# First batch of an attention + MLP kernel: LN1's scale spread over the partitions in f32 instead of as split bf16, with the start-up work around it reordered

## The chip, the cores and the metric

The kernel runs on one core of one Trainium2 chip. The metric is the device time of one execution, in microseconds. The core has five engines that work through queues of their own and wait for each other by semaphores: TensorE (PE, matmuls; PEld is its weight load), VectorE (DVE), ScalarE (ACT), GpSimd (POOL) and SyncE (SP). [...] POOL's queue also issues most of the DMAs.

## The reference

Grouped-query attention (8 batches, 16 query heads, 4 key heads, 384 rows, 64 columns a head) is followed by an affine residual MLP over 1024 columns:

```python
attn = softmax(q @ k.T / sqrt(64)); x = (attn @ v) with heads side by side   # [8, 384, 1024]
a1 = alpha1 * x + beta1
tok = einsum('ts,bsd->btd', w_tok, a1)
u = x + lam * tok
a2 = alpha2 * u + beta2
ch = relu(a2 @ w_ch1) @ w_ch2          # 1024 -> 4096 -> 1024
out = u + lam * ch
```

## The kernel before, in words

**Stages.** Each batch has a *side* (attention, the token product `tok`, and the transpose of the result, `ut`) and a *main* part (the channel MLP: 32 column blocks `nt` of the first product `h`, line 399, then the second product `ch`, line 426). Batch 0's side runs alone at the start, up to 42 us. From then on the side of batch b + 1 is woven into the main part of batch b.

**Batch 0's side.** It is a list of small steps, built at lines 359 to 382: `scores(i)` for i = 0 to 17, and after each of them what the table `at` names for that i. The order written there is the order of the instructions on every engine's queue. `scores(i)` puts one 128 x 1024 block of q times k into a PSUM tile (tag "sc", two of them) and ACT takes its exponential (line 211). `av(p)` multiplies with v for a pair of heads p, and DVE normalises (`rinv`, `x`) and scales with `g1` (line 246), which gives `a1`. `tok(p)` multiplies `a1` with the transposed `w_tok`, adds a product `R` x `H` that carries beta, and DVE adds x (line 265). `ut(p)` transposes to `a2T`, and ACT empties that. PSUM tags "tp" and "av" have one buffer each and serve all the transposes, spreads and `rows_r`; "mm" has two.

**The vectors.** alpha1, beta1, alpha2 and lam come as rows of 128 columns on eight partitions, four copies of them (`rows_f`, 32 partitions, lines 471 to 473). alpha1 and beta1 are multiplied with lam (line 509). To copy a row to all 128 partitions, a matmul with a selector is used. For bf16 matmuls without loss, `split` (lines 505 to 517) takes each f32 row apart into three bf16 parts, one in each group of eight partitions, in five DVE operations (cast, subtract, cast, subtract, cast) that wait for one another. `spread` (line 313) is then four bf16 matmuls and one copy to `vecs`. `g1` is lam * alpha1, spread in two halves: `lower` for the first four column blocks, `upper` for the others. `fill_h` (line 520) lays lam * beta1's parts out as `H`, and `rows_r` (line 303) makes the row sums of `w_tok` as `R`.

**Loads.** `loads` (line 543) names the step of batch 0's side after which POOL's queue issues a load: after step 9 the fifth tile of W1 and the first half of W2's first 512 columns (2 MB of bf16), after step 20 the next k (on SP), after step 30 the next q, after step 37 the next v. A W1 tile is loaded again five tiles ahead (`RING`), when PE is done with the one whose place it takes; W2 otherwise comes in pieces during batch 0's main part (lines 413 to 417) and stays.

**The first product's evacuation in batch 0.** The product carries one more column, from which DVE takes the bias (line 405) of every block; then ACT (even blocks) or DVE (odd blocks) writes relu(h + bias) to `hT`. The first four blocks are begun inside batch 0's side (`h_part`), two to a PSUM tile.

The table of the order, as it was:

```python
at = {1: [(warmup, 3), (split, 0, 2, 0)], 2: [(q_transpose, 2, 2, "DVE", "av"), (split, 0, 2, 1)],
      3: [(spread, lower, (0, 1), "tp"), (wtok_transpose, 0, "av")],
      4: [(av, 0), (wtok_transpose, 1, "tp"), (wtok_transpose, 2, "av")], 5: [(fill_h,), (rows_r, "tp")],
      6: [(av, 1), (q_transpose, 4, 2)], 7: [(tok, 0), (k_transpose, 2)],
      8: [(av, 2), (spread, upper, (0, 1), "av")], 9: [(tok, 1), (ut, 0)], 10: [(av, 3), (ut, 1)],
```

The functions that the change touches:

Of the kernel before, what the change touches and what calls it, by code (L numbers as in the profile page):

```python
# [12 lines left out]
def kernel(  # L13
# [21 lines left out]
    nc = tc.nc  # L35
    f32 = mybir.dt.float32
# [3 lines left out]
    MUL = mybir.AluOpType.mult  # L40
    ADD = mybir.AluOpType.add

    B, Hq, S, D = q.shape
# [4 lines left out]
    P = 128  # L48
# [4 lines left out]
    NP = Hq // 2  # L53
# [3 lines left out]
    RING = 5  # L57
# [6 lines left out]
    psum = ST(tc.psum_pool(name="psum", bufs=2))  # L64
# [6 lines left out]
    g1, h1, al2, lam_t = (vecs[:, i] for i in range(4))  # L71
# [50 lines left out]
    def load_w1(n):  # L122
        if n < B * NCH:
            t = sb.tile([P, NDT, CW * P], bf, tag="w1", name="w1", bufs=RING)
            c = n % NCH
            nc.gpsimd.dma_start(out=t, in_=w1src[:, :, c * CW * P:(c + 1) * CW * P])  # L126
            w1_tiles[n] = t

    def load_w2(dw, i, n):
        r, cs = slice(i * NNT // n, (i + 1) * NNT // n), slice(dw * 512, (dw + 1) * 512)  # L130
        nc.gpsimd.dma_start(out=w2[:, r, cs], in_=w2src[:, r, cs])
# [6 lines left out]
    def evac(eng):  # L138
        return nc.scalar.copy if eng == "ACT" else nc.vector.tensor_copy
# [16 lines left out]
    def side(b):  # L156
# [156 lines left out]
        def spread(ps_, vs, tag, eng="DVE"):  # L313
# [3 lines left out]
            for i, p in enumerate(ps_):  # L317
# [2 lines left out]
            evac(eng)(out=vecs[:, vs[0]:vs[1], ps_[0] * P:(ps_[-1] + 1) * P].rearrange("p v (n d) -> p n v d", n=n),  # L320
                      in_=ps[:, :n * w].rearrange("p (n v) d -> p n v d", n=n))

        us = []

        def add(f, *a):
# [36 lines left out]
        lower, upper = range(NP // 2), range(NP // 2, NP)  # L362
        def av(p):
            av_piece(p, 0)
            av_piece(p, 1)

        ut = a2_transpose
        at = {1: [(warmup, 3), (split, 0, 2, 0)], 2: [(q_transpose, 2, 2, "DVE", "av"), (split, 0, 2, 1)],
              3: [(spread, lower, (0, 1), "tp"), (wtok_transpose, 0, "av")],
              4: [(av, 0), (wtok_transpose, 1, "tp"), (wtok_transpose, 2, "av")], 5: [(fill_h,), (rows_r, "tp")],  # L370
              6: [(av, 1), (q_transpose, 4, 2)], 7: [(tok, 0), (k_transpose, 2)],
              8: [(av, 2), (spread, upper, (0, 1), "av")], 9: [(tok, 1), (ut, 0)], 10: [(av, 3), (ut, 1)],
              11: [(q_transpose, 6, 2), (tok, 2)], 12: [(tok, 3)], 13: [(av, 4), (ut, 2)], 14: [(ut, 3)],
              15: [(tok, 4), (av, 5)], 16: [(ut, 4)], 17: [(av, 6), (tok, 5)]}
        for i in range(18):
            add(scores, i)
# [11 lines left out]
    def main(b):  # L388
        a2T = a2Ts[b % 2]
        x = xs.pop(b)  # L390
        n = S + 1 if b == 0 else S
        for c in range(NCH):
            w1 = w1_tiles.pop(b * NCH + c)
            for j in range(CW):
                nt = c * CW + j
                begun = b == 0 and nt in early
                ps = early[nt] if begun else psum.tile([P, 512], f32, tag="mm", name="h", bufs=2)
                for dt in range(0 if begun else NDT):
                    nc.tensor.matmul(out=ps[:, :n], lhsT=w1[:, dt, j * P:(j + 1) * P],  # L399
                                     rhs=a2T[:, dt, :n], start=(dt == 0), stop=(dt == NDT - 1))  # L400
                    if dt == 3:
                        yield T_H
                c1 = bias1[:, nt:nt + 1]
                if b == 0:
                    nc.vector.tensor_copy(out=c1, in_=ps[:, S:n])
                if nt % 2 == 0:
                    nc.scalar.activation(out=hT[:, nt, :], in_=ps[:, :S], func=RELU, bias=c1)  # L407
                else:
                    nc.vector.tensor_scalar(out=hT[:, nt, :], in0=ps[:, :S], scalar1=c1,  # L409
                                            scalar2=0.0, op0=ADD, op1=mybir.AluOpType.max)  # L410
                yield T_H
            load_w1(b * NCH + c + RING)
            if b == 0 and 2 <= c < 12:
                load_w2(*((0, 6 + c, 16) if c < 10 else (1, c - 10, 16)))
            if b == 0 and c == 12:
                for i in range(1, 8):
                    load_w2(1, i, 8)
        for dw in range(NDW):
            cs = slice(dw * 512, (dw + 1) * 512)
            for ms in range(NST):  # L420
                ps = psum.tile([P, 512], f32, tag="mm", name="ch", bufs=2)
                o = sb.tile([P, 512], f32, tag="tmp", name="o", bufs=4)
                last = (b, dw, ms) == (B - 1, NDW - 1, NST - 1)
                for lo, hi in ((0, 256), (256, 384), (384, 512)) if last else ((0, 512),):
                    for nt in range(NNT):
                        nc.tensor.matmul(out=ps[:, lo:hi], lhsT=hT[:, nt, ms * P:(ms + 1) * P],  # L426
                                         rhs=w2[:, nt, dw * 512 + lo:dw * 512 + hi], start=(nt == 0), stop=(nt == NNT - 1))
                        if nt % 4 == 3 and nt < NNT - 1:
                            yield T_C
                    c = slice(dw * 512 + lo, dw * 512 + hi)  # L430
                    nc.vector.tensor_tensor(out=o[:, lo:hi], in0=ps[:, lo:hi], in1=lam_t[:, c], op=MUL)  # L431
                    nc.vector.tensor_tensor(out=o[:, lo:hi], in0=o[:, lo:hi], in1=x[:, ms, c], op=ADD)  # L432
                    nc.sync.dma_start(out=out[b].rearrange("(p st) d -> p st d", st=NST)[:, ms, c], in_=o[:, lo:hi])
                yield T_C
# [4 lines left out]
    with tc.manual_schedule(engines=order):  # L439
# [12 lines left out]
        rows_f = hTf[:32, 9216:10240].bitcast(f32)  # L452
        rows_t = hTf[:32, 10240:11264].bitcast(f32)
        rows_b = hTf[:, 11264:11776]
# [5 lines left out]
        ident_f = hTf[:, 11776:12032].bitcast(f32)  # L460
        R = stage[:, 2120:2312].bitcast(bf)
        H = stage[:, 2312:2824].bitcast(bf)
        ones = stage[:, 2824:2840].bitcast(bf)
        masks = [stage[:32, 2840 + i:2841 + i] for i in range(3)]
        sel4 = stage[:32, 2844:2848].bitcast(bf)
# [5 lines left out]
        for i, ap in enumerate((moe_alpha1, moe_beta1, moe_alpha2, moe_lam)):  # L471
            nc.sync.dma_start(out=rows_f[:, i * P:(i + 1) * P],  # L472
                              in_=bass.AP(tensor=ap.tensor, offset=ap.offset, ap=[[0, 4], [P, NP], [1, P]]))
# [28 lines left out]
                nc.vector.tensor_reduce(out=t[:n], in_=ident[:n, :n].rearrange("p (k c) -> p c k", c=NP), op=ADD, axis=AX)  # L502


        def split(lo, hi, step=None):
            c = slice(lo * P, hi * P)
            if lo == 0 and step != 1:
                r = rows_f[:, c].rearrange("p (v d) -> p v d", v=2)
                nc.vector.tensor_tensor(out=r, in0=r, in1=rows_f[:, None, 3 * P:].to_broadcast([32, 2, P]), op=MUL)
            for i, m in enumerate(masks[:2]):  # L510
                if step in (None, i):
                    src, dst = (rows_t, rows_f) if i else (rows_f, rows_t)
                    nc.vector.tensor_copy(out=rows_b[:32, c], in_=src[:, c])
                    nc.vector.scalar_tensor_tensor(out=dst[:, c], in0=rows_b[:32, c], scalar=m, in1=src[:, c],
                                                   op0=MUL, op1=mybir.AluOpType.subtract)
            if step != 0:
                nc.vector.tensor_copy(out=rows_b[:32, c], in_=rows_f[:, c])


        def fill_h():  # L520
            nc.vector.tensor_tensor(out=H[:32].rearrange("p (n d) -> p n d", n=NP),
                                    in0=rows_b[:32, None, P:2 * P].to_broadcast([32, NP, P]),
                                    in1=sel4[:, :, None].to_broadcast([32, NP, P]), op=MUL)

        place_k(0, 0)
        for h, cp in ((0, nc.vector.tensor_copy), (2, nc.scalar.copy)):
# [13 lines left out]
        def late_loads():  # L540
            load_k(1)

        loads = {9: [(load_w1, RING - 1), (load_w2, 0, 0, 2)], 20: [(late_loads,)], 30: [(load_q, 1)], 37: [(load_v, 1)]}
        for i, f in enumerate(side(0)):
            f()
            for g, *a in loads.get(i, []):
                g(*a)
# [60 lines left out]
```

The softmax here doesn't subtract the row's maximum and nothing guards it: scores larger than these inputs give would overflow.

## Time and profile before

| What | us |
|---|---|
| Median of 8 runs (814.94 to 817.23) | 815.49 |
| The profiled execution | 815.17 |
| Its span, first to last instruction | 813.3 |
| PE busy in the span | 798.5 |
| DVE / ACT / POOL busy | 348.5 / 225.2 / 186.1 |
| Last matmul of `h_part`, end of batch 0's side | 42.0 |
| First matmul of `ch`, line 426 | 90.5 |

The profile is of one execution. Its span leaves out what lies before the first and after the last instruction, here 1.87 us. Busy times of engines overlap and don't add up. A line of the timeline gives start, length, engine, source line, operation, what is written and read, shapes, a count where neighbours are merged, and in brackets how long the engine had stood before and who released it. "Granted clock" is the share of TensorE's full clock that was given to it; 1.00 is full, 0.50 half.

### The profile page before, as it was taken

The numbers are of one execution on the slowest core, as the hardware profiler recorded it, in microseconds if no ns is written. First come the engines' busy times: TensorE is split into PE (matmuls) and PEld (weight loads), VectorE is DVE, ScalarE is ACT, GpSimd is POOL, SyncE is SP. The second block draws the span as 40 slices with busy tenths as digits, with TensorE's granted clock in tenths as the row PEclk, the third lists the DMA queues.
The fourth block names the chain that finished last, engine by engine and source line by source line (L and its number), as shares of the span: only waits on it lengthen the run. The fifth ranks groups of instructions, "written<-read, shape, count | busy, mean of one in ns | idle before, by whom it ended". The sixth has DMA issues, their size and how long they took to land.

```text
span 813.3 us, 14117 instructions
## 1 busy us (share of the span) xinstructions
PE 798.5 (98%) x6090; PEld 451.8 (56%) x6144; DVE 348.5 (43%) x678; ACT 225.2 (28%) x298; POOL 186.1 (23%) x230
## 2 busy tenths in 40 slices
PE   7999999999999999999999999999999999999997
PEld 4756555565556655566455654556555565456545
DVE  7655553344443444334452444424444244442122
ACT  4654330432113321233103331034211432102100
POOL 7244430224003240123301341022500321003000
PEclk8999999999999999999999999999999999999999
DMA  9999999999259992799947999489994998129611
GB/s 176 200 197 201 202 211 139 162 176 168 54 133 176 171 148 61 138 181 173 120 93 129 179 172 91 112 131 171 178 80 100 165 172 120 36 65 194 80 39 39
DMA packets 260670, 112.57 MB, mean 138 GB/s; under 512 B 109568, under 2 KB 254464, under 8 KB 260608
## 3 DMA queue, kind: packets, MB, share of 16 engines
q0 software_dynamic: 197760, 83.28, 90.7%
q1 hardware_dynamic: 62304, 28.00, 14.4%
q8 instruction: 48, 0.79, 0.4%
q10 hardware_dynamic: 544, 0.39, 0.2%
q14 instruction: 14, 0.11, 0.0%
HBM read 170.53 MB, written 12.58 MB: 225 GB/s over the span
## 4 chain that ended last, share of the span: by engine, by line
PE 94%; DVE 4%; issue 1%; DMA 0%; SPq 0%; ACT 0%; DVEq 0%; ACTq 0%
PE ch L426 41%; PE h L399 39%; PE av L236 5%; PE sc L202 4%; PE tok L258 4%; DVE hT L409 1%; DVE x L242 1%; PE h L150 1%; DVE a1f L249 0%; DVE a L251 0%; DMA hT<-in_moe_lam_dram 0%; PE ut L275 0%; ACT hT L407 0%; SPq L472 0%; PE vec L318 0%
## 5 line engine op out<-in xcount | busy, mean ns | idle before, releaser
L399 PE MATMUL h<-a2T,w 128*128 128x384 bf16 (+1 forms) x2016 | 349.8, 326 | 1.5 <-ACT hT L407 0.5
L426 PE MATMUL ch<-w,hT 128*128 128x512 bf16 (+2 forms) x1546 | 346.1, 370 | 4.4 <-issue 1.0
L399 PEld LDWEIGHTS <-w 128*128 128x128 bf16 x2016 | 189.4, 98 | 126.1 <-issue 9.6
L126 POOL DMA_DIRECT2D w<-in_moe_w_ch_dram x128 | 112.6, 880 | 542.7 <-PE h L399 500.0
L426 PEld LDWEIGHTS <-hT 128*128 128x128 bf16 x1600 | 146.1, 98 | 153.0 <-issue 5.8
L211 ACT ACTIVATE es<-sc 128x1024 bf16<-128x1024 f32 x126 | 123.4, 1021 | 283.2 <-PE sc L202 283.2
L409 DVE TENSOR_SCALAR hT<-h,bias 128x384 bf16<-128x384 f32 x128 | 79.0, 617 | 187.1 <-PE h L399 186.5
L407 ACT ACTIVATE hT<-h,bias 128x384 bf16<-128x384 f32 x128 | 74.4, 581 | 221.4 <-PE h L399 202.4
L431 DVE TENSOR_TENSOR o<-ch,vecs 128x512 f32<-128x512 f32 (+2 forms) x50 | 33.3, 667 | 91.1 <-PE ch L426 91.1
L265 DVE TENSOR_TENSOR x<-tok,x 128x384 f32<-128x384 f32 x64 | 35.5, 555 | 80.5 <-PE tok L258 76.9
L236 PEld LDWEIGHTS <-es 128*128 128x128 bf16 x1008 | 45.8, 97 | 20.5
L236 PE MATMUL av<-v,es 128*128 128x65 bf16 x1008 | 49.0, 193 | 0.0
L202 PE MATMUL sc<-qT,kT 64*128 64x384 bf16 (+2 forms) x576 | 45.9, 274 | 0.4 <-ACT hT L211 0.3
L258 PEld LDWEIGHTS <-wtokT 128*128 128x128 bf16 x576 | 37.8, 98 | 12.6 <-issue 0.6
L241 DVE RECIPROCAL rinv<-av 128x6 f32<-128x6 f32 x64 | 12.4, 193 | 69.0 <-PE av L236 68.6
L258 PE MATMUL tok<-a,wtokT 128*128 128x128 bf16 x504 | 37.3, 219 | 0.0
L242 DVE TENSOR_TENSOR x<-av,rinv 128x384 f32<-128x384 f32 x64 | 35.7, 557 | 2.3
L202 PEld LDWEIGHTS <-kT 64*128 64x128 bf16 x576 | 20.0, 94 | 28.9 <-issue 24.8
L432 DVE TENSOR_TENSOR o<-o,x 128x512 f32<-128x512 f32 (+2 forms) x50 | 35.0, 700 | 1.7
L269 DVE TENSOR_TENSOR a<-x,vecs 128x384 bf16<-128x384 f32 x56 | 31.4, 561 | 1.9
L251 DVE TENSOR_TENSOR a<-a1f,vecs 128x384 bf16<-128x384 f32 x56 | 31.2, 558 | 2.2
L249 DVE TENSOR_TENSOR a1f<-x,vecs 128x384 f32<-128x384 f32 x56 | 31.2, 558 | 1.9
(69 smaller groups left out, 211.5 us busy)
## 6 DMA issues: line engine op xcount, KB each, us to landing
w<-in_moe_w_ch_dram POOLq DMA_DIRECT2D x135, 512.0 KB, 7.4
out_dram<-o SPq DMA_DIRECT2D x47, 256.0 KB, 2.1
q_raw<-in_q_dram POOLq DMA_DIRECT2D x21, 256.0 KB, 8.5
kst<-in_k_dram SPq DMA_DIRECT2D x16, 192.0 KB, 2.7
w<-in_moe_w_ch_dram POOLq DMA_DIRECT2D x10, 256.0 KB, 11.8
w<-in_moe_w_ch_dram POOLq DMA_DIRECT2D x1, 2048.0 KB, 21.0
v<-in_v_dram POOLq DMA_DIRECT2D x21, 64.0 KB, 8.1
a2T<-a SPq DMA_TRANSPOSE x48, 4.1
```

The lines of the kernel that those rows point to most:

```text
L126: nc.gpsimd.dma_start(out=t, in_=w1src[:, :, c * CW * P:(c + 1) * CW * P])
L202: nc.tensor.matmul(out=sc[:, hh, k % 4:k % 4 + n], lhsT=kT[r, sk, 2 * p // G, :], rhs=qT[r, st:st + n, p, :], start=True, stop=True)
L211: nc.scalar.activation(out=e, in_=sc, func=EXP, scale=scale_qk)
L236: nc.tensor.matmul(out=av[:, hh, sq, :], lhsT=ess[k // 4][:, hh, k % 4, :], rhs=vb[:, sk, hk, :], start=(sk == 0), stop=(sk == NST - 1))
L242: nc.vector.tensor_tensor(out=x[:, :, cols(p)].rearrange("p st (h d) -> p h st d", h=2), in0=av[:, :, :, :D], in1=rinv.to_broadcast([P, 2, ...
L258: nc.tensor.matmul(out=ps[:, tt, :], lhsT=wtokT[:, st, tt * P:(tt + 1) * P], rhs=a1s[p][:, st, :], start=(st == 0), stop=(st == NST - 1 an ...
L265: nc.vector.tensor_tensor(out=u, in0=ps, in1=u, op=ADD)
L399: nc.tensor.matmul(out=ps[:, :n], lhsT=w1[:, dt, j * P:(j + 1) * P], rhs=a2T[:, dt, :n], start=(dt == 0), stop=(dt == NDT - 1))
L407: nc.scalar.activation(out=hT[:, nt, :], in_=ps[:, :S], func=RELU, bias=c1)
L409: nc.vector.tensor_scalar(out=hT[:, nt, :], in0=ps[:, :S], scalar1=c1, scalar2=0.0, op0=ADD, op1=mybir.AluOpType.max)
L426: nc.tensor.matmul(out=ps[:, lo:hi], lhsT=hT[:, nt, ms * P:(ms + 1) * P], rhs=w2[:, nt, dw * 512 + lo:dw * 512 + hi], start=(nt == 0), sto ...
L432: nc.vector.tensor_tensor(out=o[:, lo:hi], in0=o[:, lo:hi], in1=x[:, ms, c], op=ADD)
```

## The change

Five things are changed, all in batch 0:

1. `g1` is spread by a new function, `spread_g1`: four f32 matmuls with an f32 selector (a column of the identity) on the product rows themselves, with no split before it. `scale_rows` is the multiplication by lam alone.
2. `split` in batch 0 takes only lam * beta1 (128 columns instead of 256), in one go, after `av(0)` instead of before the first spread. The second batch still calls it for alpha2 and lam.
3. `fill_h` is made in two halves, after scores(5) and scores(8). `rows_r` and `k_transpose(2)` come after scores(7), before `tok(0)`; `tok(0)` after scores(8); other steps of the table shift by one place; the warm-up matmuls come after scores(0) instead of scores(1).
4. The bias copy of the first product alternates between ACT (even blocks) and DVE (odd blocks).
5. W2's first load is a quarter of the rows of its first 512 columns (1 MB) instead of half of them; the second quarter is issued after step 34, behind the next q and v, which were issued after steps 30 and 37.

```diff
+        def spread_g1(ps_, tag):
+            ps = psum.tile([P, 4, P], f32, tag=tag, name="vec", bufs=1)
+            for i, p in enumerate(ps_):
+                nc.tensor.matmul(out=ps[:, i], lhsT=ident_f[:NP, p:p + 1].to_broadcast([NP, P]),
+                                 rhs=rows_f[:NP, :P], start=True, stop=True)
+            nc.vector.tensor_copy(out=g1[:, ps_[0] * P:(ps_[-1] + 1) * P], in_=ps.rearrange("p n d -> p (n d)"))
...
-        at = {1: [(warmup, 3), (split, 0, 2, 0)], 2: [(q_transpose, 2, 2, "DVE", "av"), (split, 0, 2, 1)],
-              3: [(spread, lower, (0, 1), "tp"), (wtok_transpose, 0, "av")],
-              4: [(av, 0), (wtok_transpose, 1, "tp"), (wtok_transpose, 2, "av")], 5: [(fill_h,), (rows_r, "tp")],
-              6: [(av, 1), (q_transpose, 4, 2)], 7: [(tok, 0), (k_transpose, 2)],
-              8: [(av, 2), (spread, upper, (0, 1), "av")], 9: [(tok, 1), (ut, 0)], 10: [(av, 3), (ut, 1)],
-              11: [(q_transpose, 6, 2), (tok, 2)], 12: [(tok, 3)], 13: [(av, 4), (ut, 2)], 14: [(ut, 3)],
+        at = {0: [(warmup, 3)], 1: [(scale_rows,)], 2: [(q_transpose, 2, 2, "DVE", "av")],
+              3: [(spread_g1, lower, "tp"), (wtok_transpose, 0, "av")], 4: [(av, 0), (split, 1, 2), (wtok_transpose, 1, "tp")],
+              5: [(wtok_transpose, 2, "av"), (fill_h, 0)], 6: [(av, 1), (q_transpose, 4, 2)],
+              7: [(k_transpose, 2), (rows_r, "av")], 8: [(tok, 0), (av, 2), (fill_h, 4)],
+              9: [(spread_g1, upper, "av"), (tok, 1)], 10: [(ut, 0), (av, 3)],
+              11: [(q_transpose, 6, 2), (tok, 2), (ut, 1)], 12: [(tok, 3)], 13: [(av, 4), (ut, 2)], 14: [(ut, 3)],
...
-                    nc.vector.tensor_copy(out=c1, in_=ps[:, S:n])
+                    evac("DVE" if nt % 2 else "ACT")(out=c1, in_=ps[:, S:n])
...
+        def scale_rows():
+            r = rows_f[:, :2 * P].rearrange("p (v d) -> p v d", v=2)
+            nc.vector.tensor_tensor(out=r, in0=r, in1=rows_f[:, None, 3 * P:].to_broadcast([32, 2, P]), op=MUL)
...
+        def split(lo, hi):
             c = slice(lo * P, hi * P)
+            src, dst = rows_f, rows_t
+            for m in masks[:2]:
+                nc.vector.tensor_copy(out=rows_b[:32, c], in_=src[:, c])
+                nc.vector.scalar_tensor_tensor(out=dst[:, c], in0=rows_b[:32, c], scalar=m, in1=src[:, c],
+                                               op0=MUL, op1=mybir.AluOpType.subtract)
+                src, dst = dst, src
+            nc.vector.tensor_copy(out=rows_b[:32, c], in_=src[:, c])
...
+        def fill_h(p):
+            nc.vector.tensor_tensor(out=H[:32, p * P:(p + 4) * P].rearrange("p (n d) -> p n d", n=4),
+                                    in0=rows_b[:32, None, P:2 * P].to_broadcast([32, 4, P]),
+                                    in1=sel4[:, p:p + 4, None].to_broadcast([32, 4, P]), op=MUL)
...
-        loads = {9: [(load_w1, RING - 1), (load_w2, 0, 0, 2)], 20: [(late_loads,)], 30: [(load_q, 1)], 37: [(load_v, 1)]}
+        loads = {9: [(load_w1, RING - 1), (load_w2, 0, 0, 4)], 20: [(late_loads,)], 34: [(load_q, 1), (load_v, 1), (load_w2, 0, 1, 4)]}
```

The prediction's steps use these lines of the kernel before: 509 to 517 (`split`), 318 (`spread`), 488 and 98 (POOL's copies of q and k into place), 521 (`fill_h`), 309 and 310 (`rows_r`), 177 (`k_transpose`), 275 (`ut`), 405 to 410 (bias and `hT`).

More of the change, by code (lines that the diff above doesn't have):

```diff
@@ L502 @@
                 nc.vector.tensor_reduce(out=t[:n], in_=ident[:n, :n].rearrange("p (k c) -> p c k", c=NP), op=ADD, axis=AX)
-        def split(lo, hi, step=None):
+        def scale_rows():
+            r = rows_f[:, :2 * P].rearrange("p (v d) -> p v d", v=2)
+            nc.vector.tensor_tensor(out=r, in0=r, in1=rows_f[:, None, 3 * P:].to_broadcast([32, 2, P]), op=MUL)
+        def split(lo, hi):
             c = slice(lo * P, hi * P)
[L507 to L523, printed above, removed]
+            src, dst = rows_f, rows_t
[9 more added lines that the diff above has]
+                                    in1=sel4[:, p:p + 4, None].to_broadcast([32, 4, P]), op=MUL)
         place_k(0, 0)
```

## The prediction

> **What bounds the kernel now.** I read the page's busy table first, then its chain of waits.
>
> ```profile
> PE 798.5 (98%) x6090; PEld 451.8 (56%) x6144; DVE 348.5 (43%) x678; ACT 225.2 (28%) x298; POOL 186.1 (23%) x230
> ...
> PE 94%; DVE 4%; issue 1%; DMA 0%; SPq 0%; ACT 0%; DVEq 0%; ACTq 0%
> ```
>
> PE is busy 98% of 813.3 us. The edit touches only work before 92 us (the first batch's attention, up to 42.0 us, and its channel MLP's first product, 42.0 to 90.5 us), so it can win only PE's idle time there and can lose only there. The view by stages shows how much there is. Its columns are the stage and its length, the busy time (and instructions) of PE, PE weight loads, DVE, ACT and POOL, the granted TensorE clock, and the DMA share and rate.
>
> ```profile
> 8.97:12.38 3.41, 1.28 (x20) 0.89 (x17) 2.83 (x7) 2.13 (x3) 3.41 (x5) 1.00 1.07 179
> 12.38:15.79 3.41, 2.76 (x33) 1.85 (x30) 2.56 (x7) 1.71 (x2) 2.61 (x5) 0.50 1.41 169
> 15.79:19.21 3.42, 3.42 (x33) 1.94 (x34) 3.23 (x6) 1.37 (x2) 3.42 (x5) 0.50 1.45 197
> 22.62:42.00 19.38, 19.36 (x267) 14.12 (x265) 12.89 (x29) 13.27 (x18) 5.67 (x6) 1.00 1.52 195
> 42.00:54.00 12.00, 11.29 (x88) 6.88 (x87) 8.28 (x24) 3.77 (x7) 5.64 (x7) 1.00 1.64 199
> ```
>
> PE idles 2.1 us of 8.97 to 12.38. The clock then stands at 0.50 until 19.21, two stretches of 3.41 us. From 22.6 to 42 PE has no gap. From 42 to 54 it idles 0.7 us. Note DVE: from 15.79 to 19.21 it is busy 3.23 of 3.42.
>
> The timeline names the early wait and its neighbours (start, length, engine, line, operation).
>
> ```profile
> 7.02 0.56 POOL L529 DMA_DIRECT2D stage<-in_moe_w_tok_dram  x1
> 7.58 0.84 POOL L488 COPY q_raw<-qh 128x768 bf16<-128x768 bf16 x1
> 7.79 0.91 DVE L509 TENSOR_TENSOR hT<-hT 32x256 f32<-32x256 f32 x1 [0.43 <-DMA hT<-in_moe_lam_dram]
> 10.87 0.47 DVE L514 SCALAR_TENSOR_TENSOR hT<-hT,stage 32x256 f32<-32x256 bf16 x1
> 11.38 0.34 DVE L517 CAST hT<-hT 32x256 bf16<-32x256 f32 x1
> 11.77 0.38 PE L318 MATMUL vec<-hT,stage 128*128 128x128 bf16 x4 [2.05 <-DVE hT L517]
> 13.92 0.20 DVE L241 RECIPROCAL rinv<-av 128x6 f32<-128x6 f32 x1 [0.78 <-PE av L236]
> 14.15 0.83 POOL L488 COPY q_raw<-qh 128x768 bf16<-128x768 bf16 x1 [0.80 <-DMA qh<-in_q_dram]
> 14.92 1.29 POOL L98 CAST k<-kst 128x384 bf16<-128x384 f32 x2
> 15.85 1.44 DVE L521 TENSOR_TENSOR stage<-hT,stage 32x1024 bf16<-32x1024 bf16 x1
> 16.16 1.81 POOL L488 COPY q_raw<-qh 128x768 bf16<-128x768 bf16 x1
> 17.79 0.60 DVE L310 SCALAR_TENSOR_TENSOR stage<-hT,stage,r 32x384 bf16<-32x384 bf16 x1
> 20.41 0.50 PE L177 MATMUL tp<-ident,k 128*128 128x128 bf16 x6
> ```
>
> The split of alpha and beta (L509 to L517) ends at 11.72, and PE stands 2.05 us for it. But afterwards DVE runs almost without a gap to 20.4, and PE waits for what DVE empties (k_transpose(2) at 20.41 for the copy of qT that ends at 20.36).
>
> **The change, part by part.**
>
> *1. Spread without split.* L509's product stays (it ends at 8.70); the five split operations leave the path. The f32 spread can start behind scores(3), at 9.72. No f32 product is in the trace. Lower bound: the four bf16 products, 0.22 us in the chain. Nearest row: f32 transposes (L275), three in about 0.45, so 0.15 each and 0.6 for four. Upper bound: their weight load (141 ns) and matmul (273 ns) end to end, 1.65 for four. I take 0.6, so PE is free at 10.3. Next on PE is wtok_transpose(0). Its weight is issued at 7.02 and lands 4.2 us later, at 11.22; before, that was hidden. So it starts at 11.25, not at about 12.15, and the gain is 0.9 us of the 2.05. Scores(4) at 11.42 and av(0) at 11.75 to 12.4 run at full clock (PE is busy about 2.5 of 8.97 to 12.38). DVE's first reciprocal comes at 12.55 (before 13.92), and with 0.23 + 0.59 + 0.58 the scaled av(0) is ready at 13.95 (before 15.40). DVE is 1.45 us ahead here.
>
> [...]
>
> *2. DVE's queue behind it.* The split of beta now stands between av(0) and the copies of wtokT 1 and 2. Behind it wait q_transpose(4) (its PSUM buffer "tp" is wtokT 1's), then scores(7) behind that on PE, and so ACT. Five operations 128 wide: at 256 wide and undisturbed (50 to 52 us) the cast takes 0.28 and the subtraction 0.47, so 1.9 us with gaps at most and 0.9 at half; I take 1.4. They fall on POOL's copies from 14.15 to 17.97. L509 shows the price of that: 0.91 where the same width takes 0.47 in L514, because POOL's copy ran until 8.42; +0.44. Bounds: 0 if none collides, and 2.7 if four operations each wait for a copy (0.83, 0.65, 0.65, 0.83, less a start). I take three collisions, 1.3. The split ends at 13.95 + 1.4 + 1.3 = 16.65.
>
> [...]
>
> Then two wtokT copies 0.65 (17.3), half of fill_h, 1.44/2 (18.05), av(1)'s three 1.40 (19.45), the copy of qT 0.57 (20.0). k_transpose(2) on PE 0.33 and 0.2 to be seen (20.6), its copy 0.58 (21.2), rows_r's two 0.54 + 0.60 and gaps (22.4). So tok(0), moved behind k_transpose(2), rows_r and scores(8), starts at 22.45, not 19.50. Then PE still has tok(0) 0.64, av(2) 0.66 and the upper spread 0.6: 24.35. Before, the same list was done at 22.11 (the chain's scores after the spread). That is **+2.25**; with no collision +0.95, with all +3.65. PE was gapless from there on, so nothing wins it back.
>
> *3. The clock.* After a stretch with PE busy 1.28 of 3.41 the clock was 0.50; it stayed so through a stretch with 2.76 and rose after a full one. Now PE has only q_transpose(4) and scores(7), 0.66 us, between 15.79 and 19.21, so I expect 0.50 from 19.21, and, PE idling again until 22.45, to 26.04 if the stretches lie as before. At half clock av takes 1.12 for 0.66 and scores 0.54 for 0.33 (about 1.65 times): of 3.6 us 1.4 are lost. Bounds 0 and 1.4, I take half, **+0.7**.
>
> *4. First product of the MLP.* Even bias copies go to ACT, one DVE wait less in front of each ACT evacuation. The chain 42.03 to 46.02 (bias, hT, bias, hT and so on) holds PE 0.36 us at the end, q's late DMA (its half of W2's 2 MB is now behind it) 0.28, and the wait at 53.19 for an ACT evacuation behind the second split 0.46. All go: **-1.1**; bounds -0.3 (only q) and -1.4 (with the 0.3 at 71.65, which stays behind DVE's own queue). An ACT copy of one column is not in the trace: 0.58 for 384 and 1.02 for 1024 columns give a floor near 0.32, 16 times, hidden because PE needs the buffer two products (2.6 us) later. If that cover were gone, up to 16 x 0.15 = 2.4 us.
>
> *5. DMA order.* W2's 2 MB becomes two halves; the second now issues after q and v. It is first read at 90.5, and the old load landed at 39.9; the same bytes are done by about 45, before the next W1 tiles. Cost 0, covered by 45 us. One more issue on POOL (about 0.9) lies before its wait for PE at 42.3.
>
> Sum: +2.25 + 0.7 - 1.1 = +1.85. Span 813.3 + 1.85 = 815.15; this execution took 815.17, 1.87 more than its span, so 817.0; the median of 8 runs is 0.32 above it, so **817.3 us**.
>
> **The rivals.**
> - *Even.* The split meets no POOL copy and the clock does not fall: +0.95 - 1.1, 815.3. [...] Against: L509.
> - *Faster, from DVE keeping pace.* If the five small operations fit into DVE's waits, PE keeps its lead: 0.9 at the first spread, and without the 0.50 clock the products between 12.38 and 19.21 (two av, rows_r, scores) save 0.46 + 0.46 + 0.56 + 0.21 = 1.7; the upper spread costs 0.4; with -1.1 that is -3.3, 812.2. It decides once tok(0) starts before 20.4, where PE was gapless. For: the clock row. Against: DVE is busy 3.23 of 3.42.
> - *Much slower.* Every split operation waits for POOL, half clock to 26.04, f32 at its upper bound (+1.05 at the upper spread, +0.15 at the lower): 3.65 + 1.4 + 1.2 - 1.1 = +5.15, 820.6.
> - *The MLP's gain fails*, as ACT's queue with exp (1.02 each) delays the bias: 2.25 + 0.7 = +2.95, 818.4.
>
> **How the numbers follow.** About 0.2% (1.6 us) is what a measurement here can tell. Forecast 0.40 (its own range 815.6 to 819.2; 0.29 slower, 0.11 same), even 0.22 (0.19 same, 0.03 faster), faster 0.17, much slower 0.14, failed gain 0.07. So slower 0.50, same 0.30, faster 0.20. The range runs from 813.4, part of the way to the faster case, to 820.2.
>
> **What would show it.** Right: wtok_transpose(0) waits for its DMA near 11.2; the split's operations lie between 14 and 17 and are longer than 0.3; tok(0) starts after 21; a clock of 0.50 near 19 to 26; the MLP's first product starts after 43.5 and PE's idle time behind it is under 0.2 in 12 us. Wrong: tok(0) before 20, or the clock at 1.00 throughout, or an f32 spread over 1.7 us.

## The result, and the profile after

| | before | after |
|---|---|---|
| Median (lowest to highest, runs) | 815.66 (814.94 to 817.47, 31) | 819.81 (818.08 to 823.50, 11) |
| The profiled execution / its span | 815.17 / 813.3 | 818.84 / 816.8 |
| Last long group of `h_part` starts (line 150) | 40.67 | 45.11 |
| First matmul of `ch` | 90.50 | 93.92 |

The changed kernel takes 1.0059 times as long as before, 95% interval 1.0049 to 1.0069. This is a ratio of means (820.64 and 815.80, so 4.84 us); by the medians the loss is 4.15 us, and the two differ because some runs lie far above the median. The forecast was 817.3, a loss of 1.8; it had the sign, and less than half of the size. In the profiled execution the side ends 4.44 us later, and the first product of the MLP, taken from the last long group of `h_part` to the first `ch` matmul, takes 48.81 instead of 49.83, 1.02 less. After that the two kernels keep step: 4.44 - 1.02 = 3.42 of the span's 3.5 us. The median lies another 0.97 above that execution, and the runs spread over 5.4 us where those of before spread over 2.5.

The page of the changed kernel, busy times and chain of waits:

```profile
PE 801.0 (98%) x6098; PEld 453.3 (56%) x6152; DVE 345.3 (42%) x663; ACT 227.9 (28%) x314; POOL 185.6 (23%) x231
...
PE 93%; DVE 3%; DMA 2%; issue 1%; ACT 0%; ACTq 0%; DVEq 0%
```

PE is still 98% busy. New in the chain is DMA with 2%, which had 0%: a weight load of PE, at 90.74 us, has waited 0.31 us for a tile of W1. That is little, but it says that the loads have come level with PE.

The timeline of the changed kernel where the loss arises (start, length, engine, line, operation, and in brackets the idle time and who ended it):

```profile
7.60 1.14 PE L452 MATMUL warm<-wtokT 128*128 128x384 bf16 x3
10.88 1.15 PE L327 MATMUL vec<-hT 8*128 8x128 f32 x8
11.97 0.35 PE L296 MATMUL tp<-ident,stage 128*128 128x128 bf16 x3
13.33 0.20 DVE L241 RECIPROCAL rinv<-av 128x6 f32<-128x6 f32 x1 [0.30 <-PE av L236]
14.62 0.84 DVE L522 CAST hT<-hT 32x128 bf16<-32x128 f32 x1
16.46 0.80 DVE L523 SCALAR_TENSOR_TENSOR hT<-hT,stage 32x128 f32<-32x128 bf16 x1
17.30 0.21 DVE L526 CAST hT<-hT 32x128 bf16<-32x128 f32 x1
17.83 0.80 PE L186 MATMUL tp<-ident,q_raw 128*128 128x128 bf16 x6 [2.79 <-DVE wtokT L299]
20.45 0.80 PE L177 MATMUL tp<-ident,k 128*128 128x128 bf16 x6 [1.29 <-DVE qT L189]
23.60 0.29 PE L262 MATMUL tok<-stage 128*128 128x128 bf16 x1 [0.30 <-DVE stage L310]
25.45 1.15 PE L327 MATMUL vec<-hT 8*128 8x128 f32 x8
```

The split of beta lies on DVE from 14.62 to 17.51, in front of the copies of wtokT. PE stands 2.79 us behind these copies, and 1.29 behind the copy of qT. The first product with R comes at 23.60; in the kernel before it came at 19.67:

```profile
19.67 0.22 PE L262 MATMUL tok<-stage 128*128 128x128 bf16 x1
```

A spread is eight f32 instructions, two for each product (its passes, below), 1.08 us in the chain (1.15 in the record); before it was 0.22. The upper one lies on the path.

The view by stages of the changed kernel (length, busy time and count of PE, weight loads, DVE, ACT, POOL, granted clock, DMA share and rate):

```profile
14.18:17.59 3.41, 0.85 (x22) 0.69 (x19) 3.27 (x7) 1.58 (x2) 3.06 (x6) 1.00 1.41 186
17.67:21.08 3.41, 1.96 (x16) 1.29 (x15) 2.66 (x7) 1.02 (x1) 1.35 (x2) 0.50 1.38 179
21.08:24.49 3.41, 3.11 (x22) 1.54 (x21) 1.70 (x3) 1.02 (x1) 0.00 (x0) 0.51 1.40 208
42.00:54.00 12.00, 11.98 (x99) 7.97 (x98) 6.42 (x16) 4.42 (x11) 3.70 (x5) 1.00 1.07 169
```

PE is busy 0.85 of 3.41 us while DVE splits; then come two stretches at half clock, from 17.59 to 24.42. Between 42 and 54 us PE has lost its idle time (0.7 before, 0.02 now): the bias copies on two engines do what they are for (bias_on_dve, below, takes this part back).

### The profile page after: what moved, and what is told of

It reads as the page before. It is cut to its first block, busy times and chain, and to the rows that moved or that the text cites. A ratio compares the mean times of both kernels' runs of the same rounds, so it can differ in the third digit from the quotient of the medians.

```text
span 816.8 us, 14136 instructions
## 1 busy us (share of the span) xinstructions
PE 801.0 (98%) x6098; PEld 453.3 (56%) x6152; DVE 345.3 (42%) x663; ACT 227.9 (28%) x314; POOL 185.6 (23%) x231
## 4 chain that ended last, share of the span: by engine, by line
PE 93%; DVE 3%; DMA 2%; issue 1%; ACT 0%; ACTq 0%; DVEq 0%
PE ch L434 41%; PE h L407 38%; PE sc L202 4%; PE av L236 4%; PE tok L258 4%; DMA w<-in_moe_w_ch_dram 2%; PE h L150 1%; DVE x L242 1%; DMA stage<-in_q_dram 1%; DVE a1f L249 0%; DVE a L251 0%; DVE hT L417 0%; PE ut L275 0%; PE tp L186 0%; PE vec L327 0%
## 6 DMA issues: line engine op xcount, KB each, us to landing
w<-in_moe_w_ch_dram POOLq DMA_DIRECT2D x2, 1024.0 KB, 14.1
```

## The experiments

Ratios are to the kernel before, run on the same chip in the same job, with 95% intervals; they compare means. Microseconds are medians with lowest and highest. The experiments stand in the order of the questions.

### Is it beta's split in DVE's queue?

**split_early**: the changed kernel, the split behind `scale_rows`, where PE waits anyway.

```diff
-1: [(scale_rows,)], ... 4: [(av, 0), (split, 1, 2), (wtok_transpose, 1, "tp")],
+1: [(scale_rows,), (split, 1, 2)], ... 4: [(av, 0), (wtok_transpose, 1, "tp")],
```

> The changed kernel with beta's split moved from behind av(0) to right behind scale_rows (after scores(1)), where DVE stood idle from 8.7 to 10.5 us in the changed kernel's profile. Theory 'DVE queue': the five operations (14.62 to 17.51, 2.9 us) no longer stand before the wtokT copies; q_transpose(4) then waits only for POOL's copy of q (15.4) and starts 2.0 to 2.4 us earlier than 17.83, tok(0)'s R product 1.5 to 2.5 us earlier than 23.60, and the median falls to 816.8 to 818.3. Rival 'f32 spread and clock': the loss lies in the two f32 spreads (2 x 0.9 us more than bf16) and in the half clock, and the split is only where PE's waiting shows: the median stays at 819 to 820.

816.38 (815.54 to 820.61), ratio 1.0018 (1.0005 to 1.0031). Two thirds of the loss, 0.41%, go, more than either reading expected. The timeline of split_early, DVE and then PE:

```profile
9.04 0.41 DVE L522 CAST hT<-hT 32x128 bf16<-32x128 f32 x1
9.48 0.34 DVE L523 SCALAR_TENSOR_TENSOR hT<-hT,stage 32x128 f32<-32x128 bf16 x1
```
```profile
15.90 0.72 PE L186 MATMUL tp<-ident,q_raw 128*128 128x128 bf16 x6
20.68 0.23 PE L262 MATMUL tok<-stage 128*128 128x128 bf16 x1 [0.68 <-DVE stage L310]
```

The same operations take 0.33 to 0.47 here, where POOL only issues DMAs, against 0.84, 0.48, 0.41, 0.80 and 0.21 beside POOL's copies; q_transpose(4) starts at 15.90 instead of 17.83, and the first product with R comes at 20.68 instead of 23.60. The side ends 3.28 us earlier than in the changed kernel (last `h_part` group at 41.83 instead of 45.11).

**split_after_wtok**: the changed kernel, the split behind the two copies of wtokT.

```diff
-5: [(wtok_transpose, 2, "av"), (fill_h, 0)]
+5: [(wtok_transpose, 2, "av"), (split, 1, 2), (fill_h, 0)]
```

> The changed kernel with beta's split moved behind the two wtokT copies only (in front of fill_h's first half). Theory 'DVE's work in sum': q_transpose(4) is free 2 us earlier, but R, and so tok(0), still come behind the same DVE operations: R moves by less than 0.6, the median by less than 1: 819.0 to 819.9. Rival 'the tp buffer': what cost the time was that the split held the wtokT copy and so q_transpose(4) and scores(7): the median falls by 2 or more, to 816.5 to 817.8.

821.06 (819.10 to 822.47), ratio 1.0059 (1.0045 to 1.0074), no different from the changed kernel. q_transpose(4) comes at 16.97 instead of 17.83, and R's product is still at 23.13. What counts is DVE's work in front of R as a sum, not the one wait that the timeline names longest. The time of this one profiled execution (821.92) says little by itself, since half clock lay from 19.3 to beyond 30.0 in it.

### Is it the half clock?

**warm_back**: the changed kernel, the warm-up matmuls behind scores(1) again.

```diff
-at = {0: [(warmup, 3)], 1: [(scale_rows,)],
+at = {1: [(warmup, 3), (scale_rows,)],
```

> The changed kernel with the three warm-up matmuls behind scores(1) again. Theory: in the changed kernel's profile they ran at half clock in front of scores(1) (1.07 us) and put the second exponential off from 8.3 to 9.3, and with it scores(3) and the lower spread (10.88 instead of about 9.9); wtok_transpose(0) starts at 11.25 instead of 11.97: 0.5 to 0.8 us faster where the clock starts late, nothing where it starts early; the median 819.0 to 819.6. Rival: hidden by DVE, unchanged, 819.7 to 820.

821.13 (818.25 to 824.01), ratio 1.0061 (1.0039 to 1.0083): not told apart from the changed kernel; the 0.5 to 0.8 us expected are not seen.

**keep_warm**: the changed kernel with matmuls of the identity, which nothing reads, in PE's two waits.

```diff
-6: [(av, 1), (q_transpose, 4, 2)], 7: [(k_transpose, 2),
+6: [(av, 1), (keep_warm, 36), (q_transpose, 4, 2)], 7: [(keep_warm, 14), (k_transpose, 2),
```

> The changed kernel with idle PE time filled: 36 matmuls of the identity by itself behind av(1) and 14 behind scores(7), whose results nobody reads; in the changed kernel's profile PE stood there from 15.0 to 17.8 and from 19.2 to 20.5. Theory 'clock': the granted clock no longer falls to 0.50 between about 17.6 and 24.4, so the side ends 1.0 to 1.5 us earlier, and the runs above 822, where the half clock lasts a stretch longer, go: median 818.0 to 818.9, highest under 821. Rival: the clock only shows the waiting and costs nothing of its own: 819.8 or more, with the same spread.

818.43 (817.56 to 818.79), ratio 1.0027 (1.0017 to 1.0037). Work added to PE makes the kernel 0.32% faster, and the runs lie within 1.2 us instead of 5.4. Its profile has half clock once, from 12.0 to 15.4, and full clock where the changed kernel had half:

```profile
12.38:15.79 3.41, 3.41 (x40) 1.91 (x39) 1.86 (x4) 1.73 (x2) 3.22 (x6) 0.56 1.48 186
19.21:22.62 3.41, 2.53 (x34) 1.64 (x30) 2.72 (x7) 1.02 (x1) 0.00 (x0) 1.00 1.38 214
```

R's product is still at 23.48, so DVE's lateness stays. Between the two profiled executions there is hardly a gain: the side ends only 0.49 earlier (44.62 instead of 45.11), and the first product of the MLP gives 0.46 of it back (49.27 instead of 48.81), waiting for W1's tiles. The profiled execution of the changed kernel, at 818.84, was one of those in which half clock cost little. Its four runs above 822 had a granted clock of 0.990 over the whole span, the eight of keep_warm 0.996 to 1.000. How long the half clock lasts isn't all: two runs of the changed kernel with 0.989 took 819.33 and 819.81. That its place counts too is the author's estimate; no run sets length and place apart.

### What does the f32 spread cost by itself?

**f32_old_order**: the order, bias and loads of before, with `scale_rows`, the split of beta early, and the two f32 spreads.

```diff
+at = {1: [(warmup, 3), (scale_rows,), (split, 1, 2)], 2: [(q_transpose, 2, 2, "DVE", "av")],
+      3: [(spread_g1, lower, "tp"), (wtok_transpose, 0, "av")],
...
+      8: [(av, 2), (spread_g1, upper, "av")],
```

> The f32 spread alone in the order of before: scale_rows and beta's split behind scores(1), everything else of the table, the bias copies and the loads as in the kernel before. Theory: PE's 2.05 us wait at the first spread shrinks by 0.4 to 0.9 (w_tok's landing), the upper spread costs 0.86 more; about even: 815.4 to 816.2 beside 815.7 of before. Rival 'f32 is the cost': the two spreads (1.08 each against 0.22) cost 1.5 us or more, 817 or more. Rival 'f32 was a good idea placed badly': 814.5 or less.

817.48 (815.51 to 821.81), ratio 1.0019 (1.0004 to 1.0034). By itself that reads as the price of f32, as the second reading has it. The question on passes and clock, below, shows that this is wrong in part.

### Why does the MLP's gain not show in the whole?

**bias_on_dve** (the changed kernel with every bias copy on DVE), **bias_alone** (the kernel before with the alternating bias) and **bias_loads** (that, and the new loads). The edit of bias_on_dve; bias_alone is its reverse, and bias_loads adds the changed `loads` table:

```diff
-evac("DVE" if nt % 2 else "ACT")(out=c1, in_=ps[:, S:n])
+nc.vector.tensor_copy(out=c1, in_=ps[:, S:n])
```

> The changed kernel with every bias copy on DVE again (part 4 undone). Theory: the alternation is worth 0.7 to 0.9 us between 42 and 60 us (0.36 and 0.46 in the prediction's step 4), so 820.5 to 820.8. Rival: the 1.05 us that the first product became shorter come from q's earlier landing alone: 819.8 to 820.0, unchanged.

> The kernel before with the alternating bias copies only. Theory: the two waits for ACT and DVE (0.36 and 0.46) go, so 0.6 to 0.9 us faster than before, 814.7 to 815.1. Rival: PE's gaps there move elsewhere, no change, 815.5 to 815.8.

> The kernel before with the alternating bias copies and the new order of the loads, nothing else. Theory: step 4 of the prediction whole, -1.1 us: 814.4 to 814.8, the q transpose of batch 1 no longer waiting for its DMA. Rival: the load order matters for something else (W2's second quarter late, W1 tiles late): 815.5 or more.

bias_on_dve: 820.50 (818.51 to 822.66), ratio 1.006 (1.0044 to 1.0077), not told apart from the changed kernel. In its profile, though, the first product takes 49.82 again (46.01 to 95.83), so in these profiles the alternating copies are worth the whole 1.02 and the new loads nothing, and the rival of its expectation falls. bias_alone: 815.68 (815.13 to 816.32), 0.9999 (0.999 to 1.0007). bias_loads: 816.38 (814.91 to 817.09), 1.0005 (0.9996 to 1.0014). Both expectations of a gain, of bias_alone and bias_loads, were missed. The view by stages of bias_alone, and then what PE's weight loads and matmuls wait for from 70 to 100 us (us in total, times, longest):

```profile
42.00:54.00 12.00, 11.99 (x95) 7.47 (x94) 7.78 (x20) 6.23 (x15) 5.46 (x7) 1.00 1.63 195
78.00:94.00 16.00, 15.55 (x144) 9.33 (x142) 8.90 (x20) 6.36 (x13) 6.42 (x9) 1.00 1.39 201
```
```profile
PEld L399 <- DMA w<-in_moe_w_ch_dram: 0.9, 2, 0.6
PE h L399 <- DMA w<-in_moe_w_ch_dram: 0.4, 1, 0.4
```

The 0.7 us are won between 42 and 54 (busy 11.99 instead of 11.29), and part of them is given back before 94 (15.55 instead of 15.95): W1's last tiles aren't there. The weight loads wait 0.9 us for them, and the matmuls' 0.4 lie inside the longer of these two waits, so the two don't add to the 1.3 of the expectation below. Before, W1's tile 15 needed 13.4 us from 73.71, so it landed near 87.1, and was needed at 87.33. The loads were a second bound right behind PE. But this is only half of the answer. The first product takes 49.20 here, still 0.63 less than before; in this execution the side ended 0.79 later than before (41.46 instead of 40.67), in the same order of steps, with half clock from 14.1 to 20.9 instead of 12.4 to 19.2.

**bias_w2late** and **bias_loads_w2late** ask that directly: W2's ten pieces, which share the queue with W1's tiles, are issued two steps later; the second also has the new loads. **early_w2late** and **f32_old_order_w2late** put the same into split_early, and into f32_old_order with the alternating bias.

```diff
-if b == 0 and 2 <= c < 12:
-    load_w2(*((0, 6 + c, 16) if c < 10 else (1, c - 10, 16)))
-if b == 0 and c == 12:
+if b == 0 and 4 <= c < 14:
+    load_w2(*((0, 4 + c, 16) if c < 12 else (1, c - 12, 16)))
+if b == 0 and c == 13:
```

> The kernel before with the alternating bias copies and W2's ten 256 KB pieces issued two W1 tiles later (after tiles 4 to 13 instead of 2 to 11, its seven 512 KB pieces after tile 13 instead of 12). Theory 'W1 arrives late': with the bias alone PE waited 1.3 us for W1's last tiles between 78 and 92 us, which ate the 0.7 won at 42 to 54; with 0.5 MB less queued ahead of W1 (2.6 us at 200 GB/s) those waits go, and the gain shows: 814.6 to 815.1. Rival: the gain was eaten by the side's start-up (its end moved from 42.0 to 42.8 us by the phase of the clock), so no change: 815.5 to 815.8, with the DMA waits gone all the same. If W2's later pieces come too late for the second product, PE waits for them after 91 us and it is slower than 816.

> The kernel before with parts 4 and 5 of the change whole (bias copies and load order) and the later W2 pieces. Theory: as bias_w2late, and q's early landing adds up to 0.28: ratio 0.9975 to 0.9990 to the kernel before. Rival: the load order gives nothing once W1 is on time, 0.9985 to 0.9995; if W2's second quarter is late again for W1, above 0.9995.

> split_early with the same later W2 pieces. Theory 'W1 arrives late': split_early's profile shows 1.2 us of PE waiting for W1's tiles; they go, and the median falls from 816.4 to 815.0 to 815.6. Rival: no change, 816.2 to 816.6.

> f32_old_order with the alternating bias copies and the later W2 pieces. If the f32 spread is even, this equals bias_w2late beside the kernel before: a ratio of 0.9980 to 0.9992. If the f32 spread costs, 0.9995 or more.

| | median | ratio |
|---|---|---|
| bias_w2late | 815.00 (814.23 to 816.61) | 0.9986 (0.9978 to 0.9995) |
| bias_loads_w2late | 814.54 (814.03 to 815.26) | 0.9982 (0.9974 to 0.9991) |
| early_w2late | 817.94 (814.85 to 820.44) | 1.0022 (1.0008 to 1.0035) |
| f32_old_order_w2late | 816.62 (814.35 to 819.22; one more run, of 1041.93, is left out) | 1.0006 (0.9993 to 1.0019) |

In all four profiles PE's waits for W1 are gone and the first product takes 48.50, 1.33 less than before; bias_alone had lost 0.70 of that to W1's tiles. In the first two kernels the gain arrives in the whole: bias_loads_w2late is faster than both kernels of the case. That the new loads add to it isn't shown (0.9982 and 0.9986, and 48.50 in both). With the f32 spread it doesn't arrive, against the expectation of early_w2late; these runs spread over 5 us.

### Passes of the f32 product, or clock?

**f32_loads_w2late** differs from bias_loads_w2late only in the f32 spreads (with beta's split alone, early, and `fill_h` in two halves). **f32_loads_again** is the same kernel, to have another execution of it profiled. **f32_loads_warm** fills PE's waits in it:

```diff
-3: [(spread_g1, lower, "tp"), ... 5: [(fill_h, 0), (fill_h, 4), (rows_r, "tp")], 6: [(av, 1), (q_transpose, 4, 2)],
+3: [(spread_g1, lower, "tp"), (keep_warm, 6), ... 5: [(fill_h, 0), (fill_h, 4), (keep_warm, 10), (rows_r, "tp")],
+6: [(av, 1), (keep_warm, 18), (q_transpose, 4, 2)],
```

> The best run so far (bias, loads, W2 later; ratio 0.9982), with only the f32 spreads for the bf16 ones, beta's split alone at entry 1 and fill_h's halves both at entry 5: the changed order of the steps is not in it. Theory f32 (each spread 1.08 for 0.22 us in the chain; the lower lies in PE's wait, the upper does not, and the early end of the wait is not kept by DVE): 0.9 us above, 815.4 to 816.3, ratio 0.9992 to 1.0002. Rival (freeing PE at 10.9 in place of 11.7 pays for it): 814.3 to 815.0, ratio 0.998.

> f32_loads_w2late unchanged, to profile another execution of it; its first profiled execution was of the lower group (813.82). Theory clock: an execution of 819 to 821 shows 0.50 in two stretches more between 15 and 30 us than the first, where the clock was 1.00 from 15.79, and PE's matmuls there at half rate; one of 814 to 817 shows it in none or one.

> f32_loads_w2late (runs in two groups, 813.8 to 816.6 and 819.3 to 820.7, median 819.41) with idle matmuls in the waits that its one profile shows: 6 behind the lower f32 spread, 10 in front of rows_r (0.56 us), 18 in front of q_transpose(4) (1.05 us). Theory clock (the upper group is executions whose clock fell to half once more): the upper group goes, median 814 to 816, ratio 0.998 to 1.000. [...]

f32_loads_w2late: 819.41, ratio 1.003 (1.0014 to 1.0046), against both expectations; its runs fall in two groups, five from 813.82 to 816.57 and seven from 819.31 to 820.65. The one profiled took 813.82, the other execution, f32_loads_again, 819.92. First the stages of the former, then of the latter:

```profile
11.90:15.31 3.41, 2.85 (x31) 1.88 (x29) 2.31 (x7) 2.04 (x2) 2.79 (x4) 0.50 1.37 160
24.49:27.90 3.41, 3.41 (x58) 2.41 (x56) 2.75 (x6) 3.04 (x5) 1.77 (x2) 1.00 1.46 201
```
```profile
14.26:17.67 3.41, 1.62 (x25) 0.93 (x25) 3.41 (x6) 1.82 (x2) 3.41 (x6) 1.00 1.40 188
17.67:21.08 3.41, 2.59 (x23) 1.99 (x23) 2.42 (x6) 1.02 (x1) 1.42 (x2) 0.50 1.36 208
21.08:24.49 3.41, 3.41 (x35) 2.72 (x33) 1.99 (x5) 1.02 (x1) 0.00 (x0) 0.50 1.45 198
24.49:27.90 3.41, 3.41 (x24) 2.56 (x23) 1.54 (x3) 1.02 (x1) 0.00 (x0) 0.50 1.45 198
27.90:31.30 3.40, 3.40 (x35) 2.14 (x35) 1.45 (x4) 2.42 (x4) 0.00 (x0) 0.50 1.26 208
```

One program, 6.1 us apart in the span (811.7 and 817.8). In the one, half clock lies in one stretch from 11.90 to 15.31, where PE waits for DVE. In the other it begins at 17.67, behind a stretch in which PE was busy 1.62, and lasts four stretches, to 31.3 (three more than the other, where two more were expected), three of them with PE busy throughout: from 24.49 to 27.90 PE gets through 24 instructions, where the other execution has 58 (not the same ones). PE's two waits in the latter's timeline around the fall, and the upper spread:

```profile
15.07 0.65 PE L306 MATMUL r<-wtokT,stage 128*32 128x384 bf16 x3 [1.08 <-DVE wtokT L299]
18.49 0.80 PE L186 MATMUL tp<-ident,q_raw 128*128 128x128 bf16 x6 [1.80 <-DVE stage L310]
23.44 2.07 PE L327 MATMUL vec<-hT 8*128 8x128 f32 x8
```

The freed PE runs ahead of DVE and then waits for it, 1.08 and 1.80 us, and the clock falls for what comes next, the upper f32 spread among it (2.07 instead of 1.15). With these waits filled (f32_loads_warm), the upper group is gone: 814.82 (813.58 to 816.56), ratio 0.999 (0.9981 to 0.9999), and in its profile the clock is 1.00 throughout:

```profile
17.67:21.08 3.41, 3.25 (x52) 2.44 (x50) 2.81 (x7) 2.05 (x2) 1.53 (x2) 1.00 1.41 205
```

So the f32 passes' own time is not the cost: the clock is. What the passes cost of their own is no more than separates 0.999 from 0.9982, whose intervals overlap. That leaves open whether the f32 spread has a share in the loss of clock; the last section has what the traces say.

**early_warm** (early_w2late with such matmuls, 10 behind the lower spread and 22 in front of k_transpose(2)) and **best_warm** (bias_loads_w2late with 34 in front of the bf16 spread and 8 in front of rows_r) put the same question to the changed order and to the order of before.

```diff
-3: [(spread_g1, lower, "tp"), ... 7: [(k_transpose, 2),
+3: [(spread_g1, lower, "tp"), (keep_warm, 10), ... 7: [(keep_warm, 22), (k_transpose, 2),
```

> The change with the split of beta behind scale_rows and W2's pieces later (ratio 1.0022 so far, medians scattered from 814.85 to 820.44), with 10 idle matmuls behind the lower f32 spread and 22 in front of k_transpose(2). Theory clock (what is left of the loss and its scatter is half clock that PE's waits bring): 815.0 to 816.3, ratio 0.999 to 1.0003, runs within 2 us. Rival f32 (the passes' own time, 0.9 us twice, stays whatever the clock): 817 to 818, ratio 1.0015 or above.

> The kernel before with the bias copies, the loads and W2's later pieces of the best run so far (ratio 0.9982), and idle matmuls of the identity in PE's two early waits: 34 in front of the first spread (its wait of 2.05 us) and 8 in front of rows_r (0.68 us). Theory (before's own half clock costs as after's does): 8.97 to 12.38 is busy, no half clock from 12.4 to 19.2, two av, rows_r and scores save up to 1.7 us less what DVE's queue takes back, so 813.2 to 814.2, ratio 0.9965 to 0.9977. Rival (DVE, busy 3.2 to 3.3 of 3.4 us there, sets the pace whatever the clock): 814.3 to 815.0, ratio as before, 0.998.

early_warm: 815.25 (814.43 to 817.94), ratio 1.0 (0.9991 to 1.0009), from 1.0022: clock again. Its runs still spread over 3.5 us, not the 2 expected, and the one of 817.94 had a granted clock of 1.000 on record, so the clock doesn't explain all of the spread. best_warm: 814.26 (813.32 to 815.87), ratio 0.998 (0.9972 to 0.9989), no different from bias_loads_w2late: the half clock of the kernel before costs nothing that can be measured, as the second reading has it: DVE is busy 3.38 of 3.42 us from 15.79 to 19.21 in best_warm's profile, PE 1.68 at a clock of 1.00.

## Why the forecast had the sign and not the size

| Step of the prediction | it said | profile after |
|---|---|---|
| 1: wtok_transpose(0) starts | 11.25 | 11.97 |
| 1: first reciprocal on DVE | 12.55 | 13.33 |
| 1: an f32 spread | 0.6 | 1.08 |
| 2: split of beta ends | 16.65 | 17.51 |
| 2: tok(0) goes on with R | 22.45 | 23.60 |
| 3: clock at 0.50 | 19.21 to 26.04 | 17.59 to 24.42 |
| 1 to 3: end of the side | +2.95 | +4.44 |
| 4: first product of the MLP | -1.1 | -1.02 |

**Right: the mechanism, and step 2 in its kind.** The split on DVE in front of the wtokT copies and R is the cause: moved away, 0.41% of 0.59% go. The split took 2.89 us where 2.7 were said, and POOL's copies stretched two of its five operations, not three: 0.84 and 0.80, where split_early has 0.41 and 0.34. The two between them took 0.48 and 0.41 (0.34 and 0.33 there).

**Wrong: step 3, "Bounds 0 and 1.4, I take half, +0.7".** The stretches were taken to lie as in the one profile of before. They don't keep their place: in the changed kernel they lay 1.6 us earlier, and two executions of f32_loads_w2late put them 6 us apart and made four of them out of one. Both the bound and the half of it were too small: filling PE's waits (keep_warm) takes the loss from 4.84 to 2.33 us by the means, 2.5 us, and from 4.15 to 2.47 by the medians, 1.7 (the two intervals leave some 1.5 to 3.8 for the 2.5). With 2.5 for 0.7 the sum is 1.85 - 0.7 + 2.5 = 3.65 against 4.84; with 1.7 it is 2.85 against 4.15. The remaining 1.2 or 1.3 is about what step 1 missed, below. In the profiled execution alone the term was not too small: q and k transposes, `rows_r` and tok(0) ran at half rate in the two stretches, but the side ends only 0.49 later than in keep_warm's, which had one such stretch of its own. The size lies in executions like the four above 822 us, of which none was profiled. The two parts overlap, since it is DVE's delay that makes PE idle; so 0.41% and 0.32% don't add.

**Too small: the f32 price of step 1, and with it the first reciprocal.** 1.08 instead of 0.6, from f32 transposes that are one instruction each; an f32 product here is two, 0.135 us each. On the path (the upper spread) that is 0.48, and with the reciprocal's 0.78 it makes 1.26 us. The reciprocal's 0.78 comes from the same spread and from PE at half rate before it: the three warm-up products took 1.14 us (0.66 in the execution of before). It isn't the spread's alone: in split_early and keep_warm, where the spread was over by 11.1, wtok_transpose(0) still came at 11.81 and 12.04, released by w_tok's DMA, and not at the 11.25 that step 1 set for it. Through the upper spread's end the profiled execution adds up: reciprocal 0.78, split 0.1, R's way 0.3, tok(0) at half rate 0.24, upper spread 0.48, 1.9 us later than said.

**Right in size by some luck: steps 4 and 5.** 1.02 came for 1.1. But the alternating copies win 1.33 (48.50 in the kernels with later W2 pieces), and 0.31 of it is lost to a late tile of W1. Step 5, "Cost 0, covered by 45 us", looked only at W2; the cover that was gone was that of W1's tiles. In bias_alone the same costs 0.70.

**The rivals.** "Much slower" (820.6) was near the time for the wrong reasons: neither did every operation of the split wait (they took 0.21 to 0.84) nor did an f32 spread reach 1.65 (1.15). "Faster, from DVE keeping pace" was to be decided by tok(0) starting before 20.4; it started at 22.80, behind a DVE that was busy 3.27 of 3.41. "Even" fell with both of its conditions: two operations of the split were stretched, and the clock fell. "The MLP's gain fails" fell too, in the profile: 1.02 us came.

Not settled: what PE must do in a stretch to keep its clock or get it back, what moves runs by 2 to 3 us at a granted clock of 1.000, and whether the changed order, with its clock kept (early_warm, 1.0), is worse than the old one (f32_loads_warm, 0.999); the intervals overlap.

## What to carry to other kernels

Freeing PE early was worth nothing here, where DVE set the pace (busy 3.27 of 3.41 us from 14.18 to 17.59, PE 0.85): PE then idled in lumps, and a clock of 0.50 followed, on work that was on the path all along. Before moving work into a queue, add up that queue up to the point where it is next needed, and where a clock of 0.50 shows anywhere in the profile, profile the same kernel several times: here its place and length changed between two executions of one kernel (11.90 to 15.31 and 17.67 to 31.3), and the sign was the spread of the runs, 5.4 us where it had been 2.5. The gain of 1.33 us on PE arrived only where the loads had that much slack (bias_alone lost 0.70 of it to W1's tiles): look up when the last tiles land against when they are read.

## What the runs showed of the hardware

- Half clock came in stretches of 3.41 us (one in f32_loads_w2late, 11.90 to 15.31; two in the changed kernel, 17.59 to 24.42; four in f32_loads_again, 17.67 to 31.3), from another point in each execution (12.38 in the kernel before).
- How busy PE was in such a stretch doesn't tell what came behind it. Seven at half clock with PE busy 3.40 us or more and no f32 spread were each followed by full clock: 15.79 to 19.21 in before, 27.90 to 31.3 in f32_loads_again, and those that began near 17.5 in bias_alone, 13.0 in split_early, 12.5 in split_after_wtok, 20.8 in bias_w2late and 14.9 in early_w2late. Five more as busy were followed by half clock again: two in f32_loads_again (21.08 to 27.90), two in early_w2late (8.03 to 14.86), one in split_after_wtok (26.16 to 29.57). Each of the five held 0.88 to 1.65 us of an f32 spread, whose products have 8 rows (8 x 128 in the record). And full clock also came behind a stretch with 2.85 of 3.41 busy (11.90 to 15.31 in f32_loads_w2late).
- Busy time alone doesn't tell when the clock fell either. In the 3.41 us in front of a fall PE was busy 0.85 (the changed kernel), 1.28 (before) and 1.62 (f32_loads_again), but 3.01 in the first execution of f32_loads_w2late, of which 1.15 was the f32 spread; f32_loads_again's stretch from 10.85 to 14.26, busy 3.14 with 1.15 of f32, kept its clock. Whether the f32 spread has a part in the falls, or in how long half clock lasts, is not shown: no run changes the spread's rows alone, to 128 for instance.
- In the changed kernel's profile the granted clock was given as 1.00 from the start to 17.5 us, though the warm-up products at 7.60 took 1.14 us for three, where they took 0.66 in before and in split_early.
- Idle matmuls paid in the changed kernel, where half clock lay on work on the path: 50 of them, 3.1 us of PE's busy time (keep_warm), took 0.32% off it. In the order of before, 42 of them won nothing (best_warm, 0.998 against 0.9982).
